# Order of ScalarE's squares, of a fold's two VectorE steps and of the first loads in an FNet and squared-ReLU kernel

## The chip, the cores and the metric

The kernel runs on one core of one Trainium2 chip. The metric is device time in microseconds of one launch; less is better. The core has TensorE (PE, matrix products into PSUM), VectorE (DVE), ScalarE (ACT), GpSimd (POOL) and SyncE (SP). Each works through its own instructions in the order in which the program gives them and waits for others by semaphores. DMA transfers are issued from the queues of SP, ScalarE and GpSimd.

## The reference, cut to what matters

```python
# x (8, 3008, 256), w_in (256, 2048), w_out (2048, 256), all float32
X = np.fft.fft(x, axis=1)
X = np.fft.fft(X, axis=2)
t = X.real.reshape(8 * 3008, 256)
h = np.maximum(t @ w_in, 0.0)
out = h * h @ w_out
```

## The kernel before, in words

**Transform.** The real part of the two-dimensional transform is built from cosine and sine products. `fold_steps` (L380) adds and subtracts mirrored rows and mirrored columns of one batch, so that fewer products are needed: `sums` (L388) adds row n and row S-n, `even_d` and `odd_d` (L398, L401) add and subtract mirrored columns, `odd` and `odds` (L404, L408) subtract the two halves of the rows and write the tile `od`, `even` writes `ev`, which goes through DRAM (`scr`) and comes back in another order (`back`). A batch is loaded in four quarters of its rows into one tile `xo`: quarters 0 and 1 directly (`direct`, L134), quarters 2 and 3 mirrored, by gathers with an index (`mirrored`, L146). All these loads are issued from GpSimd's queue. `z_steps` (L501) multiplies the folded rows with the cosine and sine tables (L521); the results are the columns `zc` and `zs`, 12,040 in all, in windows of up to 512 columns (25 windows, `wins`).

**Feed-forward.** The transform along d is merged into the weights: `gh` holds w_in times the cosine table, times the sine table, and the latter with a factor of about -2. For each pair of feature blocks, called a step s (8 steps in a window), P = gh0 zc and Q = gh1 zs. A column and its mirrored partner need relu(P + Q)^2 and relu(P - Q)^2. There are two ways to compute them:

- An *unchanged* step: `pq` (L779) makes P + Q in PSUM; `square(s, 0)` (L791) takes the Relu on ScalarE (L793) and squares it, on ScalarE (L796) if the step is in the plan's second list (`by_act`), else on VectorE (L798); `turn` (L786) adds -2Q in PSUM (L789); `square(s, 1)` takes Relu and square of the partner, always with VectorE's L798.
- A *halved* step (called changed in the title of the change: its copy is of -2Q): `half_q` (L804) makes Q alone (L808); ScalarE copies -2Q to `sn` (L816); `half_p` (L818) adds P in the same PSUM tile (L822), which can't begin before the copy has read it; ScalarE copies P + Q to `hd` (L824). VectorE then works on pairs of steps: row weights (L832), `sn` += them (L836), `hd` + `sn` (L846), Relu (L847), square into `h2` (L848).

PSUM has two tiles `ph` of two banks, used in turn. `h2` (two buffers) feeds the second product of the *next* window: `ffn2_steps` (L645) has 16 jobs of 8 matmuls (L662), two of which are put into each step; after some of them ScalarE copies PSUM to `osb` (L677) and SP stores it.

**Order.** The order is written by hand. Each window has a plan (`PLAN`, L60, chosen in `plan`, L714): which steps are halved, in groups, and which unchanged steps square on ScalarE. "Main" windows, in which a batch's fold is finished, halve (0,1), (3,4), (6) and square on ScalarE in steps 2, 5, 7; plans 5 and 6 halve from step 0 on and square on ScalarE in (5), 6, 7; plan 4 halves (1,2), (4,5) and squares in 0, 3, 6. The window loop (L734) lists for each step s what else is done there (`at[s]`): in main windows (L756) `load` of the next batch at step 0, `odd_d` at step 1, `odds` at step 2. In a step the order of issue is: `half_q` with its copy, waiting VectorE work, `others(s)` (L851: `at[s]`, two jobs of the second product with their `osb` copy, z work), `half_p` with its copy; or, in an unchanged step, `pq`, Relu and Square, `others(s)`, `turn`, Relu.

**Start.** Before the first window: tables by ScalarE's sine (L311 on), the first batch's loads (L149 to L169), its fold in two halves (L573 to L582), z (L583 on), the merged weights (`gh_half`).

Of the kernel before, what the change touches and what calls it, by code (L numbers as in the profile page):

```python
# [9 lines left out]
F16 = mybir.dt.float16  # L10
I32 = mybir.dt.int32
AF = mybir.ActivationFunctionType
ALU = mybir.AluOpType

HS = 32.0
P = 128
R = 6


def rev_dim(ap, i):  # L20

    dims = [list(d) for d in ap.ap]
    step, cnt = dims[i]
    dims[i] = [-step, cnt]
    return bass.AP(tensor=ap.tensor, offset=ap.offset + step * (cnt - 1), ap=dims)
# [3 lines left out]
def kernel(  # L29
# [14 lines left out]
    nc = tc.nc  # L44
# [9 lines left out]
    NFC = F // P  # L54
    WN = 512
# [29 lines left out]
    while g < TOT:  # L85
        n = min(FIRST[len(wins)] if len(wins) < len(FIRST) else WN, TOT - g)
        wins.append((g, n))
        g += n
    NW = len(wins)
# [27 lines left out]
    h2p = ctx.enter_context(tc.tile_pool(name="h2p", bufs=2))  # L117
# [8 lines left out]
    def load_x(i):  # L126
        b = bs[i]
        t = xp.tile([P, 4, R, D], F16, name="xo", tag="xo")
        o = b * S * D

        def flat(q):
            return t[:, q, :, :].rearrange("p c d -> p (c d)")

        def direct(q0, q1):  # L134
            nc.gpsimd.dma_start(
                out=t[:, q0:q1, :, :].rearrange("p q c d -> p q (c d)"),
                in_=bass.AP(tensor=x.tensor, offset=x.offset + o + (q0 * H - 5) * D, ap=[[XW, P], [H * D, q1 - q0], [1, XW]]))

        def gather(q, idx, base):
            nc.gpsimd.indirect_dma_start(  # L140
                out=flat(q), out_offset=None,
                in_=bass.AP(tensor=x.tensor, offset=0, ap=[[XW, B * S * D // XW], [1, XW]]),
                in_offset=bass.IndirectOffsetOnAxis(ap=idx, axis=0),
                element_offset=base)

        def mirrored(q):  # L146
            gather(q, idx["r" if q == 3 or b + 1 < B else "c"][:, 0:1], o + ((S if q == 2 else H) - R * (P - 1)) * D)

        if i == 0:  # L149
            direct(0, 1)  # L150
            yield t
        elif b > 0:
            direct(0, 2)
        else:

            gather(0, idx["f"][:, 0:1], o + D)
            nc.gpsimd.dma_start(out=t[0:1, 0, R - 1, :], in_=bass.AP(tensor=x.tensor, offset=x.offset + o, ap=[[D, 1], [1, D]]))
            direct(1, 2)

        mirrored(2)  # L160
        if i == 0:
            direct(1, 2)
        if b + 1 == B:

            nc.gpsimd.dma_start(
                out=t[1:2, 2, :, :].rearrange("p c d -> p (c d)"),
                in_=bass.AP(tensor=x.tensor, offset=x.offset + o + (S - R) * D, ap=[[XW, 1], [1, XW]]))
        mirrored(3)
        yield t  # L169
# [42 lines left out]
    def small(shape, name):  # L212
        return const.tile(shape, F32, name=name)
# [83 lines left out]
    ab = fop.tile([P, 2, 2, R, 130], F16, name="ab")  # L297
    nc.vector.memset(ab[:, 1, :, :, 0:1], 0.0)
    nc.vector.memset(ab[:, :, :, :, 129:130], 0.0)
    turn2 = small([P, 1], "turn2")  # L300
    nc.vector.tensor_scalar(out=turn2, in0=dvec, scalar1=0.0, scalar2=2.0, op0=ALU.is_equal, op1=ALU.mult)
    nc.vector.tensor_scalar(out=turn2, in0=turn2, scalar1=-2.0, scalar2=None, op0=ALU.add)
# [15 lines left out]
    def phase_d(sc):  # L318

        pv = ps_z.tile([P, 512], F32, name="pv", tag="pz")  # L320
        v = pv[:, 0 : 2 * P + 2].rearrange("p (c f) -> p c f", c=2)
        for c in range(2):
            nc.tensor.matmul(v[:, c], drow[:, c * P : (c + 1) * P], fcos if sc else fsin, start=(c == 0), stop=True, skip_group_check=True)
        return v, td[:, sc], dgs[1], D, c_all if sc else s_n, wd if sc else -wd
# [33 lines left out]
    d = [phase_d(0), phase_d(1)]  # L358
    sine(*a[1])
    whole(*a[2])  # L360
    q = RQ.index(1)
# [18 lines left out]
    def fold_steps(i):  # L380
        t = xs.pop(i)
# [5 lines left out]
        def sums(a=0, b=2, eng=nc.vector):  # L387
# [3 lines left out]
            nc.vector.tensor_tensor(cs[:, a:b, :, 1:D], t[:, a:b, :, 1:D], rev_dim(rev_dim(m[:, :, :, 1:D], 2), 3), op=ALU.add)  # L391
            eng.tensor_tensor(ab[:, 0, a:b, :, 0:1], t[:, a:b, :, 0:1], rev_dim(m[:, :, :, 0:1], 2), op=ALU.add)

        def load():
            if i + 1 < B:
                xs[i + 1] = next(load_x(i + 1))
# [42 lines left out]
        def fold8(sg):  # L439
            if sg == 0:  # L440
                xt = st["xt"] = fop.tile([P, 2, 2, 2, 260], F16, name="xt", tag="xt")
                yt = st["yt"] = fop.tile([P, 2, 2, 2, 130], F16, name="yt", tag="yt")
                folded[i, 1] = (xt, yt)
            rb = st["rb"]
            nc.vector.tensor_tensor(st["xt"][:, sg], rb[:, 0:2], rev_dim(rb[:, 2:4], 2), op=ALU.subtract if sg else ALU.add)
# [18 lines left out]
            nc.gpsimd.tensor_copy(spn[:, 1, :, 0:1], yt[:, 0, 0, :, 128:129])  # L464

        late = [lambda: fold8(0), lambda: fold8(1), lambda: fold16(0), lambda: (fold16(1), nyq8())]
        return {"sums": sums, "load": load, "even_d": even_d, "odd_d": odd_d, "odd": odd, "odds": odds, "nyq": nyq, "even": even, "back": back, "late": late}

    gh = const.tile([P, 3, F], F16, name="gh")

# [96 lines left out]
    def run(*jobs):  # L567
        for j in jobs:
            j()

    f0s = fold_steps(0)
    z0 = z_steps(need[0][0], late=True)
    f0s["sums"](0, 1, nc.gpsimd)  # L573
    f0s["even_d"](0, 1)
    nc.gpsimd.dma_start(out=wout16, in_=moe_w_out.rearrange("(c p) o -> p c o", p=P))
    f0s["odd_d"](0, 1)
    f0s["sums"](1, 2, nc.gpsimd)
    f0s["load"]()
    f0s["even_d"](1, 2)
# [119 lines left out]
    def fold_jobs(i):  # L699
        f = folds[i] = fold_steps(i)  # L700
        return [f["sums"], f["even_d"], f["load"], f["odd_d"], f["odds"], f["nyq"], f["even"], f["back"]]
# [5 lines left out]
    NST = NFC // 2  # L707
# [19 lines left out]
    def halved(w):  # L727

        return plan(w)[0]

    ROT = [0]
    jobs_of = {}
    old = None
    for w in range(NW):  # L734
        g0, wn = wins[w]
        h2 = h2p.tile([P, NFC, 2 * WN], F16, name="h2", tag="h2")
# [3 lines left out]
        at = [[] for _ in range(NST)]  # L740
        post = [[] for _ in range(NST)]
        if w == 0:
            at[7] = [f0s["back"]]
        elif w == 1:
            fj = fold_jobs(1)
            at = [fj[0:1], fj[1:3], fj[3:4], fj[4:5], [], [], [], []]
            post[5] = fj[5:6]
            lo, hi = 6, 7
        elif w == 2:
            te = table_steps()  # L750
            l8 = f0s["late"]
            at = [[folds[1]["even"], lambda: te["freq"](), lambda: te["args"](0)], [lambda: te["turns"](0), row_weights, l8[0]],
                  [lambda: te["mods"](0), l8[1]], [lambda: te["absm"](0), lambda: te["sins"](0)], [lambda: te["coss"](0), l8[2]],
                  [lambda: te["weigh"](), l8[3]], [], []]
            at[7].append(folds[1]["back"])
        elif w in fold_at:  # L756
            fj = jobs_of.pop(fold_at[w])
            at = [fj[2:3], fj[3:4], fj[4:5], [], [], [], fj[6:7], fj[7:8]]
            post[6] = fj[5:6]
        elif w == win_of(col_of[1, 1]) - 1:  # L760
            for st in range(4):
                at[st] = folds[1]["late"][st : st + 1]
            lo = 4
# [4 lines left out]
        if w in first_at:  # L768
            fj = jobs_of[first_at[w]] = fold_jobs(first_at[w])
# [21 lines left out]
        def square(s, sg):  # L791
            h1 = h1p.tile([P, 2, 512], F16, name="h1", tag="h1")
            nc.scalar.activation(h1[:, :, 0:wn], phs[s][:, :, 0:wn], AF.Relu)  # L793
            hv = rev_dim(h1[:, :, 0:wn], 2) if sg else h1[:, :, 0:wn]
            if sg == 0 and s in by_act:
                nc.scalar.activation(h2[:, 2 * s : 2 * s + 2, 0:wn], hv, AF.Square)  # L796
                return []
            return [lambda: nc.vector.tensor_tensor(h2[:, 2 * s : 2 * s + 2, sg * wn : (sg + 1) * wn], hv, hv, op=ALU.mult)]  # L798

        two = {s: g for g in halved(w) for s in g}  # L800
# [3 lines left out]
        def half_q(s):  # L804
            ph = phs[s] = ps_h.tile([P, 2, 512], F32, name="ph", tag="psh")
            for a in range(2):
                f0 = (2 * s + a) * P
                nc.tensor.matmul(ph[:, a, 0:wn], gh[:, 1, f0 : f0 + P], zsw[:, 0:wn], start=True, stop=True)  # L808
            g = two[s]
            if s == g[0]:  # L810
                i = ROT[0] % 2
                ROT[0] += 1
                sns[g] = const.tile([P, 2 * len(g), WN], F16, name=f"sn{i}", tag=f"w16_{i}")
                hds[g] = tmp.tile([P, 2 * len(g), 2 * WN], F16, name="hd", tag="tt")
            i = 2 * g.index(s)
            nc.scalar.activation(sns[g][:, i : i + 2, 0:wn], ph[:, :, 0:wn], AF.Copy, bias=0.0, scale=-2.0)  # L816

        def half_p(s):  # L818
            ph, g = phs[s], two[s]
# [64 lines left out]
        ng = 2 if w == 0 or wins[w - 1][1] < 384 < wn else 1  # L884
# [92 lines left out]
```

## Time and profile before

| | us |
|---|---|
| median of 3 runs | 597.76 (597.53 to 597.79) |
| the profiled execution | 598.18 |
| its span, first to last instruction | 596.4 |
| TensorE busy | 573.8 (96%) |
| VectorE busy | 534.4 (90%) |
| ScalarE busy | 514.2 (86%) |
| GpSimd busy | 120.8 (20%) |

The mean granted TensorE clock is 0.996 of full speed. In a row of the timeline stand start and duration in us, engine, line, operation, tile written and tiles read, shape, how many instructions are merged, and in brackets how long the engine was idle before it and what ended that. In the list of waits stand the waiting engine and line, the work that ended the wait, the total in us, how often, and the longest. In the table by stretches stand the stretch, its length, the busy time of each engine with the number of instructions, the granted clock, the DMA share and GB/s.

### The profile page before, as it was taken

To read this page: it belongs to the slowest core of one execution; us is meant where nothing else is said; L and a number is where in the kernel's file an instruction comes from. 1 tells how busy PE (TensorE), PEld (TensorE's weight loads), DVE (VectorE), ACT (ScalarE), POOL (GpSimd) and SP (SyncE) were. 2 spreads that over 40 slices of the span, in tenths; PEclk is the share of its full clock that TensorE was granted. 3 is DMA by queue.
4 is the path that set the end of the run, shared out by engine and by line. 5 is a ranking of instruction groups with operands and counts; after the bars stand their busy time and mean duration, and the time that the engine had idled before them with its cause. 6 is when DMAs were issued, how large, how long until landed. Compare 5 with 4: busy or idle time off the path is not lost.

```text
span 596.4 us, 11364 instructions
## 1 busy us (share of the span) xinstructions
PE 573.8 (96%) x4338; PEld 417.8 (70%) x4338; DVE 534.4 (90%) x790; ACT 514.2 (86%) x665; POOL 120.8 (20%) x153
## 2 busy tenths in 40 slices
PE   5899999999999999999999999999999999999996
PEld 2557876776776777776777767777677777777786
DVE  4796989799999999999989999899998899999990
ACT  7598988888998998989899889889899898998882
POOL 6480311302141023030411303303010210100000
PEclk9899999999999999999999999999999999999999
DMA  8948252563457227634276424655133451324222
GB/s 135 206 111 155 42 97 39 66 146 97 53 59 149 80 80 107 99 122 46 42 136 105 89 40 49 132 100 95 47 38 68 86 84 40 54 51 45 63 58 68
DMA packets 37646, 50.42 MB, mean 85 GB/s; under 512 B 4599, under 2 KB 30759, under 8 KB 37591
## 3 DMA queue, kind: packets, MB, share of 16 engines
q0 software_dynamic: 10464, 25.03, 32.0%
q1 hardware_dynamic: 26899, 24.44, 13.7%
q8 instruction: 34, 0.56, 0.4%
q10 hardware_dynamic: 228, 0.21, 0.1%
q14 instruction: 21, 0.17, 0.1%
HBM read 33.63 MB, written 27.84 MB: 103 GB/s over the span
## 4 chain that ended last, share of the span: by engine, by line
PE 39%; DVE 22%; ACT 20%; issue 10%; DMA 4%; SPq 3%; POOL 1%; ACTq 0%; DVEq 0%; POOLq 0%
PE po L662 22%; ACT h L793 8%; PE ph L822 5%; DVE h L848 5%; ACT sn L816 4%; DVE hd L846 4%; PE ph L808 4%; DVE sn L836 4%; DVE hd L847 3%; SPq L641 3%; DVE hd L832 3%; ACT hd L824 3%; PE pz L521 2%; ACT osb L677 2%; DMA out_dram<-osb 2%
## 5 line engine op out<-in xcount | busy, mean ns | idle before, releaser
L662 PE MATMUL po<-wout,h 128*128 128x256 f16 (+1 forms) x3024 | 361.6, 273 | 0.0
L662 PEld LDWEIGHTS <-h 128*128 128x128 f16 (+1 forms) x3024 | 296.6, 98 | 71.3 <-DVE h L848 0.2
L793 ACT ACTIVATE h<-ph 128x1024 f16<-128x1024 f32 (+3 forms) x158 | 151.4, 988 | 3.4 <-PE ph L784 2.0
L824 ACT ACTIVATE hd<-ph 128x1024 f16<-128x1024 f32 (+3 forms) x113 | 111.9, 991 | 34.5 <-PE ph L822 30.0
L848 DVE TENSOR_TENSOR h<-hd 128x4096 f16<-128x4096 f16 (+7 forms) x65 | 126.0, 1938 | 3.2
L816 ACT ACTIVATE sn<-ph 128x1024 f16<-128x1024 f32 (+3 forms) x113 | 111.8, 990 | 0.6 <-PE ph L808 0.6
L836 DVE TENSOR_TENSOR sn<-sn,hd 128x2048 f16<-128x2048 f16 (+7 forms) x65 | 68.1, 1048 | 15.6 <-ACT sn L816 11.0
L822 PE MATMUL ph<-zc,gh 128*128 128x512 f16 (+3 forms) x226 | 65.1, 369 | 8.1 <-ACT sn L816 7.5
L846 DVE TENSOR_TENSOR hd<-hd,sn 128x2048 f16<-128x2048 f16 (+7 forms) x65 | 67.8, 1043 | 5.3 <-ACT hd L824 2.9
L847 DVE TENSOR_SCALAR hd<-hd 128x4096 f16<-128x4096 f16 (+7 forms) x65 | 68.4, 1052 | 1.9
L832 DVE TENSOR_SCALAR hd<-eb,wv 128x512 f16<-128x512 f16 (+3 forms) x226 | 65.0, 344 | 5.3 <-DMA eb<-zs 5.2
L796 ACT ACTIVATE h<-h 128x1024 f16<-128x1024 f16 (+3 forms) x64 | 65.0, 1015 | 2.0
L808 PE MATMUL ph<-zs,gh 128*128 128x512 f16 (+3 forms) x226 | 65.1, 370 | 0.0
L798 DVE TENSOR_TENSOR h<-h 128x1024 f16<-128x1024 f16 (+3 forms) x94 | 59.8, 668 | 4.4 <-ACT h L793 4.0
L677 ACT ACTIVATE osb<-po 128x512 f32<-128x512 f32 (+3 forms) x95 | 54.3, 575 | 8.7 <-PE po L662 7.8
L783 PE MATMUL ph<-zc,gh 128*128 128x512 f16 (+3 forms) x158 | 58.4, 370 | 0.6 <-ACT h L879 0.3
L784 PE MATMUL ph<-zs,gh 128*128 128x512 f16 (+3 forms) x158 | 58.5, 370 | 0.0
L789 PE MATMUL ph<-zs,gh 128*128 128x512 f16 (+3 forms) x158 | 44.7, 370 | 0.2
L624 POOL DMA_DIRECT2D eb<-zs x23 | 16.5, 718 | 130.9 <-ACT zs L530 76.0
L808 PEld LDWEIGHTS <-gh 128*128 128x128 f16 x226 | 21.9, 97 | 24.6
L822 PEld LDWEIGHTS <-gh 128*128 128x128 f16 x226 | 20.7, 97 | 17.3 <-issue 12.0
L784 PEld LDWEIGHTS <-gh 128*128 128x128 f16 x158 | 15.4, 97 | 17.5 <-issue 1.0
(139 smaller groups left out, 419.1 us busy)
## 6 DMA issues: line engine op xcount, KB each, us to landing
out_dram<-osb SPq DMA_DIRECT2D x77, 128.0 KB
xo<-in_x_dram POOLq DMA_DIRECT2D x6, 768.0 KB, 12.3
scr<-ev POOLq DMA_DIRECT2D x8, 390.0 KB, 3.7
eb<-zs POOLq DMA_DIRECT2D x19, 128.0 KB, 7.4
rb<-scr POOLq DMA_DIRECT2D x16, 130.0 KB, 3.8
xo<-in_x_dram POOLq DMA_DIRECT2D x3, 384.0 KB, 4.8
out_dram<-osb SPq DMA_DIRECT2D x12, 94.0 KB
w<-in_moe_w_in_dram POOLq DMA_DIRECT2D x2, 512.0 KB, 11.2
```

The source lines that it names most:

```text
L662: nc.tensor.matmul(po[0:m, j * D : (j + 1) * D], h2[:, fc, q : q + m], wout16[:, fc, :], start=(fc == 0 and (j == 0 or not four or i > 3)) ...
L784: nc.tensor.matmul(ph[:, a, 0:wn], gh[:, 1, f0 : f0 + P], zsw[:, 0:wn], start=False, stop=True)
L793: nc.scalar.activation(h1[:, :, 0:wn], phs[s][:, :, 0:wn], AF.Relu)
L808: nc.tensor.matmul(ph[:, a, 0:wn], gh[:, 1, f0 : f0 + P], zsw[:, 0:wn], start=True, stop=True)
L816: nc.scalar.activation(sns[g][:, i : i + 2, 0:wn], ph[:, :, 0:wn], AF.Copy, bias=0.0, scale=-2.0)
L822: nc.tensor.matmul(ph[:, a, 0:wn], gh[:, 0, f0 : f0 + P], zcw[:, 0:wn], start=False, stop=True, skip_group_check=True)
L824: nc.scalar.activation(hds[g][:, i : i + 2, 0:wn], ph[:, :, 0:wn], AF.Copy, bias=0.0, scale=1.0)
L832: nc.vector.tensor_scalar(out=hd[:, a, :], in0=eb[w][:, 0:wn], scalar1=wv[:, 2 * g[0] + a : 2 * g[0] + a + 1], scalar2=None, op0=ALU.mult)
L836: return [lambda a=a: row(a) for a in range(2 * len(g))] + [lambda: nc.vector.tensor_tensor(sn, sn, hd, op=ALU.add)]
L846: lambda: nc.vector.tensor_tensor(rev_dim(hd[:, :, wn : 2 * wn], 2), hd[:, :, 0:wn], sn[:, :, 0:wn], op=ALU.add),
L847: lambda: nc.vector.tensor_scalar(out=hv, in0=hv, scalar1=0.0, scalar2=None, op0=ALU.max),
L848: lambda: nc.vector.tensor_tensor(h2[:, 2 * g[0] : 2 * g[-1] + 2, 0 : 2 * wn], hv, hv, op=ALU.mult),
```

## The change

Three edits.

1. A Square on ScalarE is put off (`late_sq`) when the next step, in this window or the next, is halved: it is issued right after that step's copy of -2Q, and so ahead of that step's `osb` and `hd` copies. In windows that take two steps at a time (`ng` 2) and ahead of unchanged steps it is issued at once, as before.
2. In main windows `load`, `odd_d` and `odds` all stand at step 0; before, they stood at steps 0, 1 and 2.
3. The first batch's quarters 0 and 1 are loaded by one instruction, followed by the gathers of 2 and 3; before, the order was 0, 2, 1, 3, with one instruction each. The half of the first fold that uses quarters 0 and 2 is folded in d first: for each quarter by itself, sums and differences of mirrored columns (`first_d`, `first_o`, tiles `fe` and `fo`, which lie in a buffer of `h2`), and then in n (`first_n`). The half with quarters 1 and 3 is folded as before.

```diff
-        if i == 0:
-            direct(0, 1)
-            yield t
-        elif b > 0:
+        if b > 0:
             direct(0, 2)
+            if i == 0:
+                yield t
         else:
...
         mirrored(2)
-        if i == 0:
-            direct(1, 2)
...
+    feo = h2p.tile([P, NFC, 2 * WN], F16, name="feo", tag="h2").rearrange("p f n -> p (f n)")
+    fe, fo = [feo[:, o : o + 2 * R * 130].rearrange("p (q c d) -> p q c d", q=2, c=R) for o in (0, 2 * R * 130)]
...
+        def first_d(q, eng):
+            h = q // 2
+            if h:
+                nc.vector.tensor_copy(t[0:1, 2, 0, :], t[0:1, 0, R - 1, :])
+            eng.tensor_copy(fe[:, h, :, 0:1], t[:, q, :, 0:1])
+            nc.vector.tensor_tensor(fe[:, h, :, 1:129], t[:, q, :, 1:129], rev_dim(t[:, q, :, 128:256], 2), op=ALU.add)
+
+        def first_o(q):
+            nc.vector.tensor_tensor(fo[:, q // 2, :, 1:129], t[:, q, :, 1:129], rev_dim(t[:, q, :, 128:256], 2), op=ALU.subtract)
+
+        def first_n(sg):
+            c = (fo if sg else fe)[:, :, :, sg:129]
+            nc.vector.tensor_tensor(ab[:, sg, 0, :, sg:129], c[:, 0], rev_dim(c[:, 1], 1), op=ALU.subtract if sg else ALU.add)
...
-    f0s["sums"](0, 1, nc.gpsimd)
-    f0s["even_d"](0, 1)
+    f0s["first_d"](0, nc.gpsimd)
+    f0s["first_o"](0)
+    f0s["first_d"](2, nc.gpsimd)
     nc.gpsimd.dma_start(out=wout16, in_=moe_w_out.rearrange("(c p) o -> p c o", p=P))
-    f0s["odd_d"](0, 1)
+    f0s["first_n"](0)
+    f0s["first_o"](2)
+    f0s["first_n"](1)
     f0s["sums"](1, 2, nc.gpsimd)
...
-            at = [fj[2:3], fj[3:4], fj[4:5], [], [], [], fj[6:7], fj[7:8]]
+            at = [fj[2:5], [], [], [], [], [], fj[6:7], fj[7:8]]
...
             if sg == 0 and s in by_act:
-                nc.scalar.activation(h2[:, 2 * s : 2 * s + 2, 0:wn], hv, AF.Square)
+                to = h2[:, 2 * s : 2 * s + 2, 0:wn]
+                late_sq.append(lambda: nc.scalar.activation(to, hv, AF.Square))
+                if ng > 1 or not (s + 1 in two if s + 1 < NST else w + 1 < NW and 0 in sum(halved(w + 1), ())):
+                    run(*late_sq)
+                    late_sq.clear()
                 return []
...
             nc.scalar.activation(sns[g][:, i : i + 2, 0:wn], ph[:, :, 0:wn], AF.Copy, bias=0.0, scale=-2.0)
+            run(*late_sq)
+            late_sq.clear()
```

More of the change, by code (lines that the diff above doesn't have):

```diff
@@ L466, in fold_steps @@
         late = [lambda: fold8(0), lambda: fold8(1), lambda: fold16(0), lambda: (fold16(1), nyq8())]
-        return {"sums": sums, "load": load, "even_d": even_d, "odd_d": odd_d, "odd": odd, "odds": odds, "nyq": nyq, "even": even, "back": back, "late": late}
+        return {"first_d": first_d, "first_o": first_o, "first_n": first_n, "sums": sums, "load": load, "even_d": even_d, "odd_d": odd_d, "odd": odd, "odds": odds, "nyq": nyq, "even": even, "back": back, "late": late}
     gh = const.tile([P, 3, F], F16, name="gh")
@@ L731 @@
     ROT = [0]
+    late_sq = []
     jobs_of = {}
```

## The prediction

> **What bounds the kernel now.** I read the page's busy shares first, then the waits of the whole span, then, wait by wait, the timeline of TensorE (PE) and ScalarE (ACT) around the changed lines, and last the first 25 us.
>
> ```profile
> PE 573.8 (96%) x4338; PEld 417.8 (70%) x4338; DVE 534.4 (90%) x790; ACT 514.2 (86%) x665; POOL 120.8 (20%) x153
> ```
>
> TensorE sets the time: nothing is gained unless its matmuls start earlier. VectorE (DVE) at 90% and ScalarE at 86% leave little room beside it. The largest wait of TensorE in the list of waits is
>
> ```profile
> PE ph L822 <- ACT sn L816: 7.5, 23, 0.5
> ```
>
> that is, 23 times the second half of a changed step (L822, `half_p`) stood until ScalarE's copy of -2Q (L816) had ended. A typical one, at the start of a window, by ScalarE's and then TensorE's rows:
>
> ```profile
> 348.93 1.06 ACT L796 ACTIVATE h<-h 128x1024 f16<-128x1024 f16 x1
> 349.89 0.58 ACT L677 ACTIVATE osb<-po 128x512 f32<-128x512 f32 x1
> 350.37 1.02 ACT L793 ACTIVATE h<-ph 128x1024 f16<-128x1024 f32 x1
> 351.28 1.02 ACT L816 ACTIVATE sn<-ph 128x1024 f16<-128x1024 f32 x1
> 352.98 1.02 ACT L824 ACTIVATE hd<-ph 128x1024 f16<-128x1024 f32 x1 [0.68 <-PE ph L822]
> 353.90 1.02 ACT L816 ACTIVATE sn<-ph 128x1024 f16<-128x1024 f32 x1
> ```
>
> ```profile
> 347.55 1.69 PE L662 MATMUL po<-wout,h 128*128 128x256 f16 x14
> 349.07 0.59 PE L789 MATMUL ph<-zs,gh 128*128 128x512 f16 x2
> 349.50 0.59 PE L808 MATMUL ph<-zs,gh 128*128 128x512 f16 x2
> 349.94 1.91 PE L662 MATMUL po<-wout,h 128*128 128x256 f16 x16
> 352.35 0.59 PE L822 MATMUL ph<-zc,gh 128*128 128x512 f16 x2 [0.51 <-ACT sn L816]
> ```
>
> The Square (L796) stands first in a chain without a break: Square, `osb`, the second Relu, the copy of -2Q; then ScalarE itself is idle for 0.68 us until L822 is through. The loss is a little more than the 0.51 us printed: matmuls overlap, and an unhindered next group starts about 0.17 us before the printed end of the last (349.07 against 347.55 + 1.69 = 349.24). So L822 could have started at 349.94 + 1.91 - 0.17 = 351.68, and 0.67 us are lost. Over 23 waits that makes 7.5 + 23 x 0.16 = 11 us, the most that the first edit can touch.
>
> **The change, part by part.**
>
> *Squares behind the next copy.* By the plan tables 33 Squares move: those of step 7 at 17 window starts, of steps 2 and 5 in the six "main" windows, two in window 9 and one each in windows 2 and 3. The others are followed by an unchanged step and stay. Nothing is added; each moved Square now stands behind the copy of the next step and ahead of that step's `osb` and `hd` copies. I replay the rows above. Back to back, a Square delays what follows by 0.96 us (348.93 to 349.89), `osb` by 0.48, a Relu or copy by 0.91 to 0.93.
>
> Window start: without the Square, `osb` waits for its matmuls (349.24) and starts at about 349.29, 0.60 earlier. The Relu waits for L789 (349.66) and `osb`: 349.77. The copy runs 350.68 to 351.70. L822 starts at 351.75 instead of 352.35. Then the Square runs from 351.59, and `hd` starts at 352.55 (L822 ends at 352.34), so 0.2 us of delay is given back. The next copy ends at 354.49, the next L822 starts at 354.54; before, that copy ended at 354.92. **0.43 us is kept of 0.67.** Four waits have these 0.51 us. Seven more at window starts are smaller, from first to last
>
> ```profile
> 160.02 0.59 PE L822 MATMUL ph<-zc,gh 128*128 128x512 f16 x2 [0.16 <-ACT sn L816]
> ...
> 541.24 0.59 PE L822 MATMUL ph<-zc,gh 128*128 128x512 f16 x2 [0.27 <-ACT sn L816]
> ```
>
> and there the same replay clears the whole loss, 0.31 to 0.45 us each, 2.9 us together. With the four: 1.7 + 2.9 = **4.6 us**. A twelfth, at 136.04, is set by late matmuls and gains nothing; at the five other window starts TensorE waits for nothing, and the 0.68 us of idle ScalarE take most of the Square.
>
> Step 2 of a main window, ScalarE and TensorE:
>
> ```profile
> 190.18 0.58 ACT L677 ACTIVATE osb<-po 128x512 f32<-128x512 f32 x1
> 190.66 1.01 ACT L793 ACTIVATE h<-ph 128x1024 f16<-128x1024 f32 x1
> 191.56 1.02 ACT L816 ACTIVATE sn<-ph 128x1024 f16<-128x1024 f32 x1
> 192.46 0.61 ACT L677 ACTIVATE osb<-po 128x512 f32<-128x512 f32 x1
> 193.26 1.02 ACT L824 ACTIVATE hd<-ph 128x1024 f16<-128x1024 f32 x1 [0.19 <-PE ph L822]
> 194.19 1.02 ACT L816 ACTIVATE sn<-ph 128x1024 f16<-128x1024 f32 x1
> ```
>
> ```profile
> 187.91 1.91 PE L662 MATMUL po<-wout,h 128*128 128x256 f16 x16
> ...
> 192.64 0.59 PE L822 MATMUL ph<-zc,gh 128*128 128x512 f16 x2 [0.21 <-ACT sn L816]
> ...
> 195.25 0.59 PE L822 MATMUL ph<-zc,gh 128*128 128x512 f16 x2
> ```
>
> Here a second `osb` stands between the copy and `hd`, and ScalarE has only 0.19 us free. `osb` can start at 189.87 (187.91 + 1.91 + 0.05), 0.31 earlier, and the copy ends at 192.27: L822 gains 0.32. But then Square from 192.16, `osb` from 193.12, `hd` from 193.60 (was 193.26), next copy 194.53 to 195.55, next L822 at 195.60 instead of 195.25. The wait moves one step on and comes out 0.35 us **worse**. Where z matmuls stand ahead of the next L822 they cover a part of it, so I take 0.25 as the mean. Six main windows: **+1.5 us**.
>
> Step 5 of a main window has no second `osb`:
>
> ```profile
> 321.80 0.59 PE L822 MATMUL ph<-zc,gh 128*128 128x512 f16 x2 [0.37 <-ACT sn L816]
> ```
>
> `osb` comes 0.30 us earlier as above, nothing is given back; five such waits: **-1.5 us**. The remaining moves (windows 2, 3, 9) have slack on both sides: nothing, or 0.35 us each at worst. Sum of the first edit: -4.6 + 1.5 - 1.5 = **-4.6 us**; the ends are -11 (every wait goes) and +9 (below).
>
> *The fold's two VectorE operations at step 0 of a main window.* `odd_d` and `odds` take 0.97 us each and move ahead of
>
> ```profile
> 306.05 1.23 DVE L836 TENSOR_TENSOR sn<-sn,hd 128x2048 f16<-128x2048 f16 x1 [1.79 <-ACT sn L816]
> ```
>
> into a hole of 1.79 us that VectorE spends waiting for a copy. They fill it and overshoot by 0.15 us; since they leave later places free, VectorE is ahead afterwards. TensorE has no listed wait on these results. I cost it at nothing; without that hole it would delay one pair of steps by 1.9 us, which has a whole window until L662 reads it. `load` stays at step 0, so POOL's and SP's queues keep their order there.
>
> *The first batch.*
>
> ```profile
> 10.85 0.21 DVE L389 COPY xo<-xo 1x256 f16<-1x256 f16 x1 [2.79 <-DMA xo<-in_x_dram,idx_r]
> ...
> 14.64 0.96 DVE L391 TENSOR_TENSOR cs<-xo 128x1530 f16<-128x1530 f16 x1 [1.51 <-DMA xo<-in_x_dram,idx_r]
> 15.64 0.57 DVE L399 TENSOR_TENSOR ab<-cs 128x768 f16<-128x768 f16 x1
> ```
>
> ```profile
> 16.94 0.65 PE L521 MATMUL pz<-cos,od 128*128 128x376 f16 x3 [4.01 <-DVE od L406]
> ```
>
> ```profile
> 1.37 0.69 POOL L135 DMA_DIRECT2D xo<-in_x_dram  x1 [0.41 <-issue]
> ...
> 4.10 0.58 POOL L135 DMA_DIRECT2D xo<-in_x_dram  x1
> ```
>
> ```profile
> DMA to landing us min/median/max: 4.9/11.3/14.3
> ```
>
> TensorE's first real work starts 2.30 us after L391 of the second half. Quarters land in the order 0, 2, 1, 3: quarter 0 at 6.3 (the shortest landing, 4.9 after the issue at 1.37), quarter 2 at 10.8, quarter 3 at 14.6. From 2 over 1 to 3 a quarter takes 1.9 us, but from 0 to 2 4.5: 2.6 us are lost where quarter 2 starts. Now 0 and 1 come by one instruction, then 2, then 3: POOL's second direct issue (0.58) is gone, so the last gather and w_in are issued that much sooner, and the DMA engines have 0 and 1 to move while the gather of 2 is written. After quarter 2 VectorE has the copy (0.25) and four operations of 0.57 us, 2.55 in all, against 0.21 + 0.96 + 2 x 0.57 = 2.31 before; the two operations on quarter 0 lie ahead of it. TensorE then starts at the later of (quarter 2 + 2.55) and quarter 3, plus 2.30. Bounds of the landing: if quarter 2 takes quarter 1's old place (14.6 - 1.9 = 12.7), VectorE is late and TensorE starts at 17.55, +0.6 us. If the quarters stream at 1.9 us each from 6.3 on, 2 lands at 10.1 and TensorE starts at 14.95, -2.0 us. I take 10.7, nearer the second, since the 2.6 us are lost at a transfer's start, which is now covered: start at 15.55, **-1.4 us**. All later loads move along; `wout16` goes behind quarter 2's copy on POOL as before.
>
> After its pause TensorE runs at half clock:
>
> ```profile
> 18.00:20.00 2.00, 1.92 (x9) 0.79 (x8) 0.18 (x1) 0.66 (x3) 1.21 (x2) 0.50 1.40 198
> 20.00:21.30 1.30, 1.30 (x5) 0.56 (x4) 0.24 (x1) 0.60 (x1) 0.00 (x0) 0.50 1.46 199
> ```
>
> (seventh figure after the window: granted clock 0.50). TensorE is busy throughout, so 3.3 us at half speed cost at most 1.6, and I take 1.2 as the part on the path. I leave this loss in: the pause shrinks from 4.0 to 2.6 us, and no row shows whether that is enough. The Trainium skill, "TensorE: Matmul & The Clock Gate", Part 1, says that the clock halves after an idle free-running window of about 3.4 us; by that rule a pause of 2.6 us halves nothing, and the sum would be 1.2 us lower. The row agrees with the halving after 4.0 us and says nothing on 2.6.
>
> **Sum.** -4.6 + 0 - 1.4 = -6.0 us: span 596.40 to 590.4. The profiled execution took 598.18 us, 1.78 around its span and 0.42 above the median of the three runs; with the same share, 597.76 - 6.0 = **591.8 us**.
>
> **Rivals.**
> - *The clock holds*, as priced: 590.6. For: the halving came after a pause of 4.0 us alone. Against: it came late, a microsecond after work had resumed, so the pause need not be the only condition. The Trainium skill's page named above has this rival's rule.
> - *The landings do not come sooner*: quarter 2 at 12 to 12.7, first edit as summed: 593.1 to 593.8. For: its landing is set by the last of 16 engines, and why that one is late the rows do not say.
> - *The wait is handed on at every moved Square*, as in the main window's step 2: the first edit comes out near zero and only the start is left, 596.4. For: Square 0.96 against 0.68 idle. Against: the window starts, where 0.43 is left after the second L822.
> - *Slower*: ScalarE's loop in changed steps (copy 1.02, L822, `hd` 0.92, again) already fills TensorE's 2.61 us per step, so a Square put inside it costs 0.96 - 0.68 = 0.28 us, and wherever the first copy cannot start sooner nothing pays for that. It decides from the point where `osb` or the Relu, not the Square, sets the copy. If that held at all 33: +9.2 - 1.4, 605.6. Against it: Square and copy stand back to back in the rows above.
> - *Every wait goes*, with the clock: 597.76 - 11 - 2.6 = 584.2; the replay speaks against it.
>
> **How the numbers follow.** Forecast 591.8 with 0.38; clock holds 590.6, 0.20; landings late 593.5, 0.15; handed on 596.4, 0.13 (half of it within 0.2%); slower 605.6, 0.08; every wait gone 584.2, 0.06. The range leaves out the last two and a little: 587.0 to 596.6. A measurement of this kernel tells about 0.2% (1.2 us) from no change: faster 0.85, same 0.07, slower 0.08.
>
> **What would show it.** The wait of L822 on L816 falls from 7.5 us to 3 or less in total; at window starts Square stands between L816 and L824, and ScalarE's idle before L824 (0.68) is gone there; in main windows a wait appears at the second L822. VectorE's 1.79 us hole ahead of L836 closes. L521 starts at about 15.5 instead of 16.94, and the clock column tells which start it was. Wrong would be: L822 waiting as long on the next step's copy, TensorE waiting on VectorE's results, or L521 at 17 or later.

## The result and the profile after

| | before | after |
|---|---|---|
| median of 5 runs, same chip | 597.53 (594.78 to 597.79) | **591.84** (591.56 to 593.33) |
| ratio, 95% interval | | 0.9911 [0.9892, 0.9931] |
| profiled execution; its span | 598.18; 596.4 | 593.33; 591.6 |
| mean granted clock in it | 0.996 | 0.995 |

The kernel is faster by 0.9%, and the time lies on the forecast, 591.8. The terms behind it do not all lie there; the sections below take them apart. Two of the five runs of before took 594.78 and 595.40 us; their clock is not on record. The busy shares after, from the page:

```profile
PE 572.6 (97%) x4338; PEld 417.2 (71%) x4338; DVE 537.5 (91%) x793; ACT 510.9 (86%) x665; POOL 116.6 (20%) x153
```

TensorE's work is the same (572.6 against 573.8 us); it only stands less. Two rows of ScalarE's waits before, and then the list of waits after:

```profile
ACT hd L824 <- PE ph L822: 30.0, 51, 1.0
...
ACT osb L677 <- PE po L662: 7.8, 27, 0.7
```

```profile
ACT osb L693 <- PE po L678: 24.9, 52, 2.0
...
ACT hd L847 <- PE ph L845: 12.7, 24, 1.0
...
PE ph L845 <- ACT sn L837: 4.2, 12, 0.6
...
PE pz L534 <- DVE od L419: 2.1, 1, 2.1
...
PE po L678 <- DVE h L871: 1.2, 1, 1.2
```

In the kernel after, L845 is `half_p` (L822 before), L829 `half_q` (L808), L837 the copy of -2Q (L816), L847 the copy to `hd` (L824), L693 the copy to `osb` (L677), L810 the Relu (L793), L814 the Square (L796), L678 the second product (L662), L855, L859, L869 and L870 VectorE's row weights, sums and Relu (L832, L836, L846, L847), L871 the squares into `h2` (L848), L534 the z matmuls (L521). ScalarE's idle time has moved from ahead of `hd` (30.0 us, now 12.7) to ahead of `osb` (7.8, now 24.9). The wait for the copy fell from 7.5 us in 23 places to 4.2 in 12, the wait before z from 4.0 to 2.1, and the last row is new.

A window start, ScalarE and TensorE, the place that the prediction replayed from before:

```profile
346.29 1.02 ACT L810 ACTIVATE h<-ph 128x1024 f16<-128x1024 f32 x1
347.19 1.03 ACT L837 ACTIVATE sn<-ph 128x1024 f16<-128x1024 f32 x1
348.09 1.07 ACT L814 ACTIVATE h<-h 128x1024 f16<-128x1024 f16 x1
349.04 1.04 ACT L847 ACTIVATE hd<-ph 128x1024 f16<-128x1024 f32 x1
349.94 1.05 ACT L837 ACTIVATE sn<-ph 128x1024 f16<-128x1024 f32 x1
```

```profile
346.46 1.91 PE L678 MATMUL po<-wout,h 128*128 128x256 f16 x16
348.27 0.59 PE L845 MATMUL ph<-zc,gh 128*128 128x512 f16 x2
```

The Square now stands between the copy and `hd`, where ScalarE idled for 0.68 us before; L845 follows L678 without a wait. Step 2 of a main window:

```profile
190.00 0.59 PE L845 MATMUL ph<-zc,gh 128*128 128x512 f16 x2
190.43 0.59 PE L829 MATMUL ph<-zs,gh 128*128 128x512 f16 x2
190.85 1.91 PE L678 MATMUL po<-wout,h 128*128 128x256 f16 x16
193.25 0.59 PE L845 MATMUL ph<-zc,gh 128*128 128x512 f16 x2 [0.49 <-ACT sn L837]
```

The first L845 has lost its wait of 0.21 us; the next one, which had none, waits 0.49, as forecast. The first fold on VectorE (L396 is the copy of a row of quarter 2, L398 to L405 the fold in d and n, L390 `sums` of the second half), and TensorE's first z:

```profile
10.34 0.22 DVE L396 COPY xo<-xo 1x256 f16<-1x256 f16 x1 [0.78 <-DMA xo<-in_x_dram,idx_r]
10.59 0.57 DVE L398 TENSOR_TENSOR feo<-xo 128x768 f16<-128x768 f16 x1
11.27 0.57 DVE L405 TENSOR_TENSOR ab<-feo 128x774 f16<-128x774 f16 x1
11.75 0.56 DVE L401 TENSOR_TENSOR feo<-xo 128x768 f16<-128x768 f16 x1
12.34 0.65 DVE L405 TENSOR_TENSOR ab<-feo 128x768 f16<-128x768 f16 x1
12.91 0.95 DVE L390 TENSOR_TENSOR cs<-xo 128x1530 f16<-128x1530 f16 x1
```

```profile
15.19 0.65 PE L534 MATMUL pz<-cos,od 128*128 128x376 f16 x3 [2.11 <-DVE od L419]
```

L390 no longer waits for quarter 3; VectorE, not the loads, now sets the start of z, 1.75 us earlier than before. The clock by stretches (seventh figure) in this execution:

```profile
16.00:18.00 2.00, 1.93 (x10) 0.85 (x8) 0.39 (x2) 0.81 (x3) 1.49 (x2) 0.54 1.24 198
18.00:20.00 2.00, 2.00 (x7) 0.80 (x6) 0.69 (x1) 0.69 (x2) 0.00 (x0) 0.60 1.46 199
```

Both profiled executions thus ran about 3.4 us at half clock, so their difference, 4.85 us, holds no gain of the clock. Last, the place of the new wait, VectorE and then TensorE near the end:

```profile
551.74 2.29 DVE L871 TENSOR_TENSOR h<-hd 128x4096 f16<-128x4096 f16 x1
553.95 1.14 DVE L855 TENSOR_SCALAR hd<-eb,wv 128x512 f16<-128x512 f16 x4
555.54 1.22 DVE L859 TENSOR_TENSOR sn<-sn,hd 128x2048 f16<-128x2048 f16 x1 [0.46 <-DVE hd L855]
556.87 1.23 DVE L869 TENSOR_TENSOR hd<-hd,sn 128x2048 f16<-128x2048 f16 x1
558.13 1.23 DVE L870 TENSOR_SCALAR hd<-hd 128x4096 f16<-128x4096 f16 x1
559.39 2.29 DVE L871 TENSOR_TENSOR h<-hd 128x4096 f16<-128x4096 f16 x1
```

```profile
561.74 1.92 PE L678 MATMUL po<-wout,h 128*128 128x256 f16 x16 [1.21 <-DVE h L871]
```

TensorE has overtaken VectorE: the last squares of window 23 end at 559.39 + 2.29 = 561.68, and the second product of the last window needs them. It has a forerunner at 549 us, where ScalarE's copy to `hd` waits for VectorE and L845 behind it 0.60 us (0.17 before):

```profile
546.85 1.02 ACT L847 ACTIVATE hd<-ph 128x1024 f16<-128x1024 f32 x1 [1.43 <-DVE h L871]
```

**Where the time went.** I set each TensorE matmul of after beside the same one of before, in order, and took the difference of the starts. It changes only at a few places:

| place | us | forecast |
|---|---|---|
| first z (16.94 to 15.19), with 0.08 more by 30 us | -1.83 | -1.4 |
| the 11 window starts that were priced (160 to 541 us in before) | -4.34 | -4.6 |
| the six other window starts | -0.55 | none |
| step 2 of six main windows | +1.55 | +1.5 |
| step 5 of five main windows | -1.53 | -1.5 |
| two shifts at 506 and 549 us | +0.55 | none |
| L678 waiting for the last squares (561.74) | +1.38 | none |
| smaller steps | +0.04 | none |
| sum | -4.73 | -6.0 |

### The profile page after: what moved, and what is told of

The parts are those of the page before. It is cut to its first block, busy times and chain, and to the rows that moved or that the text cites. A ratio compares the mean times of both kernels' runs of the same rounds, so it can differ in the third digit from the quotient of the medians.

```text
span 591.6 us, 11374 instructions
## 1 busy us (share of the span) xinstructions
PE 572.6 (97%) x4338; PEld 417.2 (71%) x4338; DVE 537.5 (91%) x793; ACT 510.9 (86%) x665; POOL 116.6 (20%) x153
## 4 chain that ended last, share of the span: by engine, by line
PE 71%; ACT 11%; DVE 8%; issue 4%; DMA 4%; SPq 1%; POOL 0%; ACTq 0%; DVEq 0%; POOLq 0%
PE po L678 41%; PE ph L845 7%; PE ph L829 5%; PE ph L800 4%; PE ph L801 4%; PE ph L806 4%; ACT sn L837 4%; PE pz L534 3%; DMA out_dram<-osb 3%; DVE h L871 2%; ACT hd L847 2%; ACT h L814 1%; ACT h L810 1%; DVE sn L859 1%; DVE hd L869 1%
## 5 line engine op out<-in xcount | busy, mean ns | idle before, releaser
L678 PE MATMUL po<-wout,h 128*128 128x256 f16 (+1 forms) x3024 | 361.7, 273 | 1.2 <-DVE h L871 1.2
L678 PEld LDWEIGHTS <-h 128*128 128x128 f16 (+1 forms) x3024 | 296.5, 98 | 72.7 <-DVE h L871 1.6
L810 ACT ACTIVATE h<-ph 128x1024 f16<-128x1024 f32 (+3 forms) x158 | 151.8, 991 | 5.1 <-PE ph L806 2.8
L871 DVE TENSOR_TENSOR h<-hd 128x4096 f16<-128x4096 f16 (+7 forms) x65 | 126.0, 1938 | 3.1
L847 ACT ACTIVATE hd<-ph 128x1024 f16<-128x1024 f32 (+3 forms) x113 | 112.3, 995 | 18.2 <-PE ph L845 12.7
L837 ACT ACTIVATE sn<-ph 128x1024 f16<-128x1024 f32 (+3 forms) x113 | 112.7, 998 | 0.6 <-PE ph L829 0.6
L693 ACT ACTIVATE osb<-po 128x512 f32<-128x512 f32 (+3 forms) x95 | 54.9, 581 | 27.3 <-PE po L678 24.9
L859 DVE TENSOR_TENSOR sn<-sn,hd 128x2048 f16<-128x2048 f16 (+7 forms) x65 | 68.1, 1047 | 11.4 <-ACT sn L837 6.5
L869 DVE TENSOR_TENSOR hd<-hd,sn 128x2048 f16<-128x2048 f16 (+7 forms) x65 | 67.9, 1044 | 5.7 <-ACT hd L847 2.8
L870 DVE TENSOR_SCALAR hd<-hd 128x4096 f16<-128x4096 f16 (+7 forms) x65 | 68.4, 1052 | 1.9
L855 DVE TENSOR_SCALAR hd<-eb,wv 128x512 f16<-128x512 f16 (+3 forms) x226 | 65.5, 345 | 4.8 <-DMA eb<-zs 4.8
L845 PE MATMUL ph<-zc,gh 128*128 128x512 f16 (+3 forms) x226 | 65.1, 369 | 4.5 <-ACT sn L837 4.2
L814 ACT ACTIVATE h<-h 128x1024 f16<-128x1024 f16 (+3 forms) x64 | 65.4, 1023 | 1.0
L829 PE MATMUL ph<-zs,gh 128*128 128x512 f16 (+3 forms) x226 | 65.1, 370 | 0.0
L829 PEld LDWEIGHTS <-gh 128*128 128x128 f16 x226 | 22.0, 97 | 24.5
L845 PEld LDWEIGHTS <-gh 128*128 128x128 f16 x226 | 20.4, 97 | 13.2 <-issue 7.2
```

The lines of the kernel that those rows point to most:

```text
L678: nc.tensor.matmul(po[0:m, j * D : (j + 1) * D], h2[:, fc, q : q + m], wout16[:, fc, :], start=(fc == 0 and (j == 0 or not four or i > 3)) ...
L814: late_sq.append(lambda: nc.scalar.activation(to, hv, AF.Square))
L845: nc.tensor.matmul(ph[:, a, 0:wn], gh[:, 0, f0 : f0 + P], zcw[:, 0:wn], start=False, stop=True, skip_group_check=True)
L847: nc.scalar.activation(hds[g][:, i : i + 2, 0:wn], ph[:, :, 0:wn], AF.Copy, bias=0.0, scale=1.0)
L859: return [lambda a=a: row(a) for a in range(2 * len(g))] + [lambda: nc.vector.tensor_tensor(sn, sn, hd, op=ALU.add)]
L869: lambda: nc.vector.tensor_tensor(rev_dim(hd[:, :, wn : 2 * wn], 2), hd[:, :, 0:wn], sn[:, :, 0:wn], op=ALU.add),
```

## The experiments

Lines in the diffs are the changed ones; `...` stands for lines left out. All ratios are to the kernel before on the same chip.

**One edit at a time.** Kernel before with the first edit alone (the `late_sq` lines of the change's diff):

> Only the put-off squares; loads, first fold and odd_d/odds as before. Theory (each site is a trade of its own): TensorE's start stays at about 16.9 us; against the kernel before, the matmuls run 4.3 to 4.8 us earlier by 560 us (window starts -0.25 to -0.65 each, step 2 of a main window +0.2 to +0.35 net, step 5 -0.3), and 1 to 1.5 us are lost again in the last windows to VectorE: 3 to 4 us less in the profiled span at the same clock state. Rival (the gain is handed on at every site): within 1 us of before. Rival (odd_d and odds at step 0 are needed for it): the moves give less than 2 us without them.

594.88 us (594.37 to 595.77), ratio 0.9950 [0.9934, 0.9967]. Matmul by matmul: -4.62 where the last window begins (-0.06 behind the start), then the same +1.37, in the end -3.24. Its waits (here L829 is `half_p`, L821 the copy of -2Q, L855 the squares):

```profile
PE ph L829 <- ACT sn L821: 4.0, 12, 0.5
...
PE po L662 <- DVE h L855: 1.2, 1, 1.2
```

So the handed-on wait of step 2 and the wait at the end both belong to the first edit.

The third edit alone (loads and fold in d):

> Only the first batch's loads and its fold in d; squares and the order in main windows as before. Theory: first z matmul at about 15.2 instead of 16.9 us, every later matmul about 1.7 us earlier, no other step in the difference to before: about 1.7 us less at the same clock state, and up to 1.7 more where the clock doesn't drop after the shorter pause. Rival (the start's gain is absorbed later by a wait that was slack): the difference shrinks along the span, under 1 us at the end.

594.68 us (594.60 to 594.72), ratio 0.9946 [0.9927, 0.9965]. z starts at 15.23, 1.71 earlier; at 21.4 us, where the half clock of before ends, the lead is 3.26, and 3.34 at the end. The 1.55 between 1.71 and 3.26 is the clock: it was granted in full here, in all four runs (0.998 to 0.999).

The second edit alone:

```diff
-            at = [fj[2:3], fj[3:4], fj[4:5], [], [], [], fj[6:7], fj[7:8]]
+            at = [fj[2:5], [], [], [], [], [], fj[6:7], fj[7:8]]
```

> Only odd_d and odds at step 0 of main windows. Theory: VectorE's hole ahead of the row sums closes, TensorE's matmuls don't move (difference to before under 0.3 us all along); time the same. Rival (VectorE bounds the main windows): 1 to 2 us either way per run, seen in TensorE's waits for VectorE or ScalarE.

597.95 us (595.74 to 598.97), ratio 0.9994 [0.9980, 1.0007]: nothing. VectorE's hole is filled, as the rows of after show where before had 1.79 us idle, but nobody waited behind it (in the trace of this run every matmul is 0.2 to 0.3 us later than before, from the first z on):

```profile
300.05 0.97 DVE L415 TENSOR_TENSOR ab<-cs 128x1536 f16<-128x1536 f16 x1
301.05 0.97 DVE L422 TENSOR_TENSOR od<-ab 128x1548 f16<-128x1548 f16 x1
301.94 1.13 DVE L855 TENSOR_SCALAR hd<-eb,wv 128x512 f16<-128x512 f16 x4
303.18 1.23 DVE L859 TENSOR_TENSOR sn<-sn,hd 128x2048 f16<-128x2048 f16 x1
```

**The third edit in its two halves.** Kernel before with the new loads and the old fold:

```diff
-        if i == 0:
-            direct(0, 1)
-            yield t
-        elif b > 0:
+        if b > 0:
             direct(0, 2)
+            if i == 0:
+                yield t
...
-        if i == 0:
-            direct(1, 2)
```

> The kernel before with the new loads alone (quarters 0 and 1 by one instruction, then the gathers of 2 and 3); the old fold, sums of quarters 0 and 2 first. Theory (the gain is the earlier landing, 10.3 and 12.2 us instead of 10.8 and 14.6; the fold in d only keeps VectorE off the path): VectorE has 2.3 us after quarter 2, is done at about 12.7 and starts the second half then: first z matmul at about 15.0 us, as with both edits (15.2). Rival (the fold in d is what gains, the loads alone only change the order): first z matmul at 16.5 or later.

594.17 us (593.71 to 596.10, 8 runs), ratio 0.9939 [0.9922, 0.9956]. The loads alone do all of it; z starts at 14.72, *earlier* than with the fold in d. VectorE's rows say why (L386 is the copy of quarter 2's row, L388 `sums`, L396 `even_d`, L399 `odd_d`):

```profile
10.24 0.21 DVE L386 COPY xo<-xo 1x256 f16<-1x256 f16 x1 [2.56 <-DMA xo<-in_x_dram,idx_r]
10.49 0.96 DVE L388 TENSOR_TENSOR cs<-xo 128x1530 f16<-128x1530 f16 x1
11.49 0.57 DVE L396 TENSOR_TENSOR ab<-cs 128x768 f16<-128x768 f16 x1
11.97 0.56 DVE L399 TENSOR_TENSOR ab<-cs 128x768 f16<-128x768 f16 x1
12.44 0.96 DVE L388 TENSOR_TENSOR cs<-xo 128x1530 f16<-128x1530 f16 x1
```

From the copy of quarter 2 to the second half it is 12.44 - 10.24 = 2.20 us here and 12.91 - 10.34 = 2.57 with the fold in d: once quarter 2 is the late one, four operations behind it cost 0.37 us more than three. (The whole times of this kernel and of the third edit alone, 594.17 and 594.68, have overlapping intervals; the rows carry the statement.)

Kernel before with the fold in d and the old order of loads:

> The kernel before with the new fold of the first half alone; loads in the old order 0, 2, 1, 3, one instruction each. Theory: quarter 3 lands at 14.4 to 14.9 us as before and sets the start: first z matmul at 16.7 to 17.3, time as before within 0.2%. Rival (fold in d gains by itself): 16.3 or earlier.

597.27 us (595.83 to 599.01, 10 runs), ratio 0.9996 [0.9983, 1.0009]: nothing, since VectorE then waits for quarter 3 at L393 all the same. Its first z, at 16.34, is earlier than expected and close to the rival's 16.3, but that is the landing and not the fold: quarter 3 is complete at 13.95 us here and at 14.55 in before, and z follows 2.39 us later in both.

**The loss in step 2.** Kernel after, where the Square of step 2 in main windows is issued at once again:

```diff
-                if ng > 1 or not (s + 1 in two if s + 1 < NST else w + 1 < NW and 0 in sum(halved(w + 1), ())):
+                if ng > 1 or (s == 2 and w in fold_at) or not (s + 1 in two if s + 1 < NST else w + 1 < NW and 0 in sum(halved(w + 1), ())):
```

> The changed kernel, but the Square of step 2 of the six main windows is issued at once, as before. Theory (there the put-off costs more than it gives): the 0.5 to 0.65 us waits at the second half_p of these windows are gone, the first one's 0.3 us wait is back: 0.2 to 0.35 us better per main window, the matmuls about 1.3 us earlier at 550 us than in the changed kernel; of that 0.5 to 1.3 us are left at the end, since VectorE sets the last windows. Rival (every put-off gains): 1 to 2 us slower than the changed kernel.

590.98 us (589.92 to 591.59), ratio 0.9879 [0.9856, 0.9901]. Against after, TensorE is 1.52 us ahead by 453 us, behind the last of the six places, and 1.84 at the end. That is more than the 0.5 to 1.3 expected there: VectorE's last squares end 1.83 us earlier too (559.85 against 561.68). The second L845 has no wait any more (192.62), the first has its old one:

```profile
190.00 0.59 PE L845 MATMUL ph<-zc,gh 128*128 128x512 f16 x2 [0.21 <-ACT sn L837]
...
192.62 0.59 PE L845 MATMUL ph<-zc,gh 128*128 128x512 f16 x2
```

**The clock.** The kernel of the last experiment with 16 matmuls on zeros ahead of the first z instead of 6, so that TensorE hardly pauses:

```diff
-    idle(6)
+    idle(16)
```

> The changed kernel with step 2 of main windows squared at once (as the run before this one), and 16 instead of 6 matmuls on zeros ahead of the first z, so that TensorE pauses for under 1 us instead of 2.1 to 2.4. Theory (the granted clock halves after a pause, at 1.4 us of loss): clock 1.00 throughout the start in every run, 1.4 us less than those runs of the same kernel that had the half clock, and times closer together: 589.5 to 590.3. Rival (the half clock comes by the time since the start, whatever TensorE does, or zeros don't count as work): half clock as often as without them, 590 to 591.6.

590.09 us (589.92 to 590.39), ratio 0.9871 [0.9847, 0.9896]; granted clock 0.999 to 1.0 in every run. Without the ten more idle matmuls two of four runs had 0.997 and 591.6 us, the other two 0.999 and 589.92 and 590.38 us. Then the same on the kernel before, with 28 instead of 6 and nothing else:

```diff
-    idle(6)
+    idle(28)
```

> The kernel before with 28 idle matmuls instead of 6, nothing else: TensorE has no pause ahead of the first z. Theory: the half clock after the start comes from that pause, so the granted clock is 0.998 or more in every run and the time is 1.4 to 1.8 less than before's: 595.9 to 596.4. Rival: the half clock comes anyway some microseconds after the start of steady work: 0.995 to 0.997 and 597.5 to 598.

596.40 us (596.02 to 596.76, 10 runs), ratio 0.9978 [0.9969, 0.9988], clock 0.999 to 1.0 in all ten. TensorE's rows of this kernel:

```profile
11.79 4.71 PE L341 MATMUL pw<-spn 128*128 128x384 f16 x28
17.01 0.65 PE L521 MATMUL pz<-cos,od 128*128 128x376 f16 x3 [0.51 <-DVE od L406]
```

z starts no earlier than before (17.01 against 16.94), and from 22 us on every matmul is 1.47 to 1.48 us earlier, so the 1.26 us to before's 597.66 on that chip are the clock alone: the pause makes the half clock, and the kernel before paid for it in nearly every run.

**The wait at the end.** Step 2's Square at once, and the next to last window planned as the last one is (its step 5 is unchanged instead of halved, and squares on ScalarE), which takes work from VectorE before the last window:

```diff
-        return PLAN[5 if first or late or w + 1 == NW else 6]
+        return PLAN[5 if first or late or w + 2 >= NW else 6]
```

> The changed kernel with step 2 of main windows squared at once, and window 23 planned as (0,1), (2,3), (4) halved with ScalarE's squares in 5, 6, 7: VectorE has some 2.8 us less in it, TensorE 0.43 more. Theory (the 1.4 us that TensorE loses ahead of a product in the last window come from VectorE, which is busy without a break there): that wait of 1.2 us for the squares of a halved pair goes; 0.6 to 1.0 us less than without this edit. Rival (the wait is one on the row sums' DMA, which stays): the wait moves and the time is the same or 0.4 us more.

588.95 us (588.84 to 590.76), ratio 0.9850 [0.9826, 0.9875]. The wait is gone. Against the kernel with step 2's Square at once, TensorE is 0.47 us later ahead of this product, since window 23 costs it more, and 0.91 us earlier from there on, as expected:

```profile
558.75 0.47 PE L829 MATMUL ph<-zs,gh 128*128 128x360 f16 x2
559.05 1.91 PE L678 MATMUL po<-wout,h 128*128 128x256 f16 x16
```

VectorE's wait for the row sums (`eb`), the rival cause, is still there in this kernel, 1.19 us at 513.58, with nothing lost by it. So less work for VectorE near the end is enough to clear TensorE's wait. That the row sums have no part in it is not shown. VectorE's row weights of one pair, in before and in after:

```profile
519.16 1.14 DVE L832 TENSOR_SCALAR hd<-eb,wv 128x512 f16<-128x512 f16 x4
```

```profile
515.27 1.14 DVE L855 TENSOR_SCALAR hd<-eb,wv 128x512 f16<-128x512 f16 x4 [1.35 <-DMA eb<-zs]
```

Ahead of them VectorE is 5.3 us earlier than before, at them 3.9, and at the last squares 4.7. This DMA takes 8.6 to 8.8 us from its issue to its landing in the six profiled executions without the first edit and 9.9 to 10.1 in the six with it, and in these alone VectorE waits for it, 1.1 to 1.4 us. No run lands the row sums sooner, so how much of the loss is theirs stays open, as does why the DMA takes longer.

**All together.** The kernel of the last experiment with the old fold behind the new loads (as in the half above that has the loads alone), and 13 idle matmuls:

```diff
-    idle(6)
+    idle(13)
...
-    f0s["first_d"](0, nc.gpsimd)
-    f0s["first_o"](0)
-    f0s["first_d"](2, nc.gpsimd)
+    f0s["sums"](0, 1, nc.gpsimd)
+    f0s["even_d"](0, 1)
...
-    f0s["first_n"](0)
-    f0s["first_o"](2)
-    f0s["first_n"](1)
+    f0s["odd_d"](0, 1)
```

> The kernel after with step 2's Square at once, the next to last window planned like the last, the direct quarters loaded by the new queues but folded by the old instructions (all in cs, none in d), and 13 idle matmuls instead of 6 so that TensorE has work up to the first z. Theory: the loads alone gave z at 14.72 where the fold in d gave 15.23, so z starts 0.5 earlier than in the kernel with the window 23 planned late, the clock holds in every run, and the rest is as there: 588.4 (588.2 to 588.7), against 588.84 to 589.0 of its full-clock runs. Rival: the half second of the start is lost at the first folds behind it (VectorE has the second half of cs later): 588.9 or more.

588.76 us (588.70 to 589.30), ratio **0.9851 [0.9837, 0.9865]**, the best version. Its ratio does not tell it from the kernel of the last experiment (0.9850, on another chip). It misses its expectation: at equal clock it is 0.1 to 0.2 us better than that kernel (588.84 to 589.00), not 0.5. z starts at 14.88: quarter 2's copy starts at 10.40, 0.16 later than with the loads alone, and that kernel had z at 15.16 in its profiled run, so only 0.28 was there to gain. From copy to z it is 14.88 - 10.40 = 4.48, as with the loads alone (14.72 - 10.24), against 15.19 - 10.34 = 4.85 with the fold in d.

## Why the prediction was right, and where it was not

- **Window starts: right.** The eleven priced places gave -4.34, forecast -4.6. The replay was right at the four large ones (0.45 kept, forecast 0.43) and a little high at the other seven (2.53 together instead of 2.9), mostly because at 495 and 541 us 0.15 came back at the next L845. Six window starts that were put at nothing gave 0.05 to 0.25 each, 0.55 together.
- **Step 2: right, in sign and size.** +0.22 four times, +0.34 and +0.35, sum +1.55. Undoing it alone gains 1.5 us. The number given for L845's remaining wait, 3 us or less, was too low: 4.2, because the six new waits of 0.23 to 0.49 us, 2.1 together, were priced in the time and forgotten in that list.
- **Step 5: right.** -1.53 against -1.5.
- **odd_d and odds: right.** Nothing, though the hole of 1.79 us closes; alone it measures 0.9994 [0.9980, 1.0007].
- **Start: right path, mis-sized by 0.35.** Quarter 2 was taken at 10.7 and its copy started at 10.34. What VectorE needs behind it (2.57 against 2.55) and TensorE behind that (2.28 against 2.30) came as worked out. The reason given for 10.7, that 2.6 us are lost at a transfer's start, does not hold: in before the first of quarter 2's 16 completions comes at 7.30 us, 1.0 after quarter 0 has landed, and only the last at 10.75. What came sooner is the last completion, so the estimate was near by luck. What I did not see is that the loads do it alone and that the fold in d then costs 0.37 us: I added its operations up, 2.55 against 2.31, and let the difference stand as part of the edit instead of asking what the loads would give with the old ones.
- **The clock: the forecast and its rival were both half right.** The loss was left in as a fact of each run; the runs show that it falls by run. In the profiled execution of after it was there, in the other four runs of that kernel it was not (clock 0.998 to 1.0, 591.56 to 592.04, against 0.995 and 593.33). Before, nearly every run had it. So most runs of after gained 1.3 to 1.8 us that the sum of -6.0 did not hold. The price of 1.2 was low: TensorE gains 1.5 where only the clock differs (1.47 in before with 28 idle matmuls, 1.55 with the third edit alone).
- **The end: missed.** "Since they leave later places free, VectorE is ahead afterwards" and "TensorE has no listed wait on these results" looked at VectorE only where the edit put its operations. The failed step is that every gain of TensorE was carried to the end of the span, though the prediction itself says at its head that VectorE at 90% leaves little room. VectorE came only 4.7 us earlier where TensorE came 6.1 earlier, and 1.38 us were handed back in the last window, after 0.42 at 549 us. TensorE waiting on VectorE's results is one of the signs that the prediction itself named as being wrong. Before, the squares there ended at 564.10 + 2.29 = 566.39 and their reader started at 566.48, without a wait but also without slack:

```profile
564.10 2.29 DVE L848 TENSOR_TENSOR h<-hd 128x4096 f16<-128x4096 f16 x1
```

That row could have been read in the profile of before. Part of VectorE's lead was lost in its wait for the row sums at 515 us, which the prediction did not look at either.

That the total is right to 0.1 us is luck, since misses cancel: 1.38 + 0.55 us lost near the end against 0.4 more at the start, 0.3 more at the window starts and the clock that held in most runs. With the half clock that the forecast assumed, the kernel took 593.33 us, 1.5 more than forecast. By the edits alone, at equal clock, it is about -4.7 us: both profiled executions at half clock give 598.18 - 593.33 = 4.85, and the runs with the clock held 596.40 (before with idle matmuls, on another chip) against 591.56 to 592.04.

Of the rivals, "the clock holds" is what most runs show, though at 591.56 to 592.04 and not at its 590.6; "landings late" is refuted by the copy at 10.34; "handed on at every Square" holds in the main windows' step 2 alone; "slower" and "every wait goes" show nowhere.

## What to carry to other kernels

Moving an in-order engine's work behind the operation that another engine waits for pays only where that work then meets idle time; replay the next two waits from the timeline, place by place, and leave it where it was if a second consumer stands in between. When the bounding engine is pulled ahead, check every producer near the end of the span for slack, and the transfers that feed it: one that ends 0.1 us before its reader gives the gain back. Take an edit of two halves apart before crediting both.

## What the runs showed of the hardware

- **Half clock by run.** By TensorE's pause ahead of the first z in the profiled execution: with 3.4 to 4.3 us (the first edit alone, the second alone, the fold in d alone) 23 of 25 runs had a mean clock of 0.997 or less, and so had 45 of the 46 runs of before that were taken beside the experiments (4.0 us). With 2.1 to 2.3 us (after and three kernels with its start) it was 4 of 17, with 1.45 us (loads alone) 1 of 8 (596.10 us against 593.71 to 594.56), with 0.3 to 0.7 us 0 of 19. In after it costs 1.3 to 1.8 us. Fourteen of the runs with the long pause had 0.993 or 0.994 and were about 1 to 2 us slower still; their traces were not kept. The Trainium skill, "TensorE: Matmul & The Clock Gate", Part 1, gives a free-running window of about 3.4 us and halving after an idle one. The half clock does last about 3.4 us here, and a part that falls by run fits a free-running window; but it also came after pauses of 2.1 and 1.45 us, shorter than a window, so a window that is only partly idle can be enough. The measurement decides.
- **How busy is busy enough.** The granted clock of all twelve traces changes only in steps of 3.41 us. Counted in these steps, from where the record of the clock starts (9.1 to 12.1 us) to the last matmuls, TensorE was busy 0.16 to 1.36 us in every step that the half clock followed (after: 1.30 us from 12.77 to 16.18), and 1.59 us or more in every other step. Where between 1.36 and 1.59 of 3.41 us the limit lies is not measured. It also shows why the run decides: after and the third edit alone pause alike, 2.11 and 2.15 us, but in the latter a step ends at 14.51, inside the pause, TensorE is busy 1.84 and 2.61 us in the two steps that share it, and the clock holds.
- **Matmuls on zeros hold the clock** as well as real ones: 28 of them in 4.71 us, then full clock.
- **A transfer's last completion.** Four quarters of the same size land sooner in the new order. By the 16 completions that the trace has for each transfer, quarter 3 is complete at 13.95 to 14.86 us in the five profiled runs with the old order and at 12.00 to 12.34 in the seven with the new, though the gather of quarter 2 is issued later there (3.25 against 3.06 us). In the old order the last completion of quarter 2 comes 2.5 to 3.5 us after the first one (before: 7.30 and 10.75), and as late for quarters 1 and 3; in the new one 0.6 to 1.0 us (after: 9.47 and 10.31). Why it falls behind when a gather follows a single quarter, the runs do not settle.
